# Another emission order for the start of a fused attention and feed-forward kernel, with new prices in its planner

## The chip, the cores and the metric

The kernel runs on one core of one Trainium2 chip. The metric is the device time of one execution in microseconds. Every time below is of the kernel before the change; "the profiled execution" is the single execution whose records the profile holds.

## What is computed

```python
# attention: q (4, 12288, 128), kv (4, 384, 32, 128), w_sr (128, 128)
kv_pool = kv.reshape(B, H // 4, 4, W // 4, 4, C).mean(axis=(2, 4))
k = v = kv_pool.reshape(B, -1, C) @ w_sr            # 768 keys a batch
s = (q @ k.transpose(0, 2, 1)) / np.sqrt(C)
s = s - s.max(-1, keepdims=True)
a = np.exp(s)
a /= a.sum(-1, keepdims=True) + 1e-09
x = (a @ v).reshape(49152, 128)
# feed-forward: w_in (128, 2048), w_out (2048, 128)
h = x @ w_in
g = h * (1.0 / (1.0 + np.exp(-1.702 * h)))
out = g @ w_out
```

Inputs and output are float32; the kernel multiplies in bfloat16. It leaves out the subtraction of the maximum and takes the row sum from a column of ones beside v.

## The kernel before

**Tiling.** The 49152 queries are 96 groups of 512, 24 groups a batch; four groups share one tile of transposed queries (qT). The 768 keys of a batch are six chunks of 128. A chunk of work on ScalarE (ACT) is 128 keys by 512 queries (exp, written to the buffer `ag`), or, in the feed-forward part, 128 hidden columns by 512 tokens (gelu). A **unit** is one ACT instruction over up to K = 3 chunks, that is three PSUM banks. Two sets of three banks (0 to 2, 3 to 5) alternate between units. The last two banks, 6 and 7, called spare here, serve everything else in turn: pooling, keys, values, transposes, and the sums that the drains collect (`acc`, `next_acc`).

**Fills and drains.** A fill (`fill_attn`, L331, or `fill_moe`, L511) is TensorE's one 512-column matmul per chunk, followed by ACT's instruction over all of them (L336 or L515). A drain of attention (`drain_attn`, L338) is K = 3 matmuls with 129 columns for one tile of 128 queries and half of the keys; three tiles (18 matmuls) share a spare bank, which VectorE (DVE) then empties with a reciprocal (L354) and a multiplication (L362). A drain of the feed-forward part (L517) is one 512-column matmul; 16 of them make a group of the output. `turn` (L418) transposes attention's output back, six tiles at a time.

**Four passes.** Attention for the first half of the groups (0 to 47), feed-forward for them, attention for the second half, feed-forward for it. Four groups of the second half (48 to 51) have their exp made on DVE from a polynomial (`early_fill`, L382 to L411) during the first feed-forward pass.

**What sets the order.** One Python loop (from L637) writes the instructions of all engines in order; each engine executes its own in that order. After the fill of unit n + 2 the loop gives TensorE drains and small jobs for the time of unit n, as far as a planner thinks that they fit: it holds a clock `now` for TensorE, the ends of ACT's units `end` (FIXED + CHUNK x chunks, L632 to L635) and, for each spare bank, when it comes free. Its unit of time is one 512-column matmul. `COST` (L607) gives each small job two numbers: what TensorE takes, and how much later the bank is free. Ahead of each fill `prepare` (L568) puts the jobs that the table `first` (L584) lists by hand for that unit, without asking whether they fit, and starts background work for groups that begin there: `background` (L453) issues `load_qT` two tiles ahead (a transposing load on SyncE's queue, SP), `cast_q` five tiles ahead, for group 10 the pixel loads of batch 1, and appends the pooling and the keys of batch 1 to the list `extras`, from which the loop takes when the planner allows. `gate` (L446) makes GpSimd's queue (POOL) wait for DVE, so that a load isn't issued earlier than its place.

**Start.** The pixel loads of batch 0 (`load_chunk`, L121, 512 KB after the cast) and the first four tiles of queries (`load_q`, L212) go through POOL's queue in the order of L232 to L243. `pool_chunk` (L128) sums 4 x 4 pixels by 16 small matmuls, `key_chunk` and `value_chunk` (L139, L146) multiply by w_sr; each ends in a DVE copy from the spare bank. `transpose_q` (L217) makes four transposes of one group of queries and a copy into qT, by ACT for group 0 and by DVE for the others. `warm` and `warm_wide` (L268, L281) are matmuls whose result nobody reads. The first eight groups are taken by key chunk and not by group, since the keys arrive one chunk at a time; the list `sizes` (L536) cuts them into units of one to three chunks.

**Frames.** `place` (L300) chooses where in `ag` a unit's result goes: in frames of three slots, and for the first eight groups in slots strided by group.

The lines of code that the steps of the prediction turn on are these:

```python
if p >= 2:
    now = max(now, end[p - 2] + HANDOVER / 2)
now += len(part)
begin = max(now + HANDOVER / 2, end[p - 1] if p else 0.0)
end.append(begin + FIXED + CHUNK * len(part))
```

Of the kernel before, what the change touches and what calls it, by code (L numbers as in the profile page):

```python
# [24 lines left out]
def kernel(  # L25
# [4 lines left out]
    _, H, W, _ = kv.shape  # L30
# [3 lines left out]
    JC = J // 128  # L34
# [7 lines left out]
    GB = NG // B  # L42
    SB = NS // B
    K = 3
# [36 lines left out]
    free = {6: 0.0, 7: 0.0}  # L81
    last_acc = 7
# [9 lines left out]
    def next_acc():  # L92
        return min((m for m in (13 - last_acc, last_acc) if m not in closes), key=lambda m: free[m])

    def acc_bf():
        return acc().bitcast(BF)
# [9 lines left out]
    def x_tile(s):  # L106
        return x[:, s % XS * SG:(s % XS + 1) * SG]
# [13 lines left out]
    def load_chunk(b, jc):  # L121

        a, ch = divmod(jc, HC)
        t = x_tile(XS - 1 - jc)
        nc.gpsimd.dma_start(out=t, in_=kv_r[b, a, ch])
        kv_tiles[b, jc] = t.rearrange("p (wp w1 c) -> p w1 wp c", w1=r, c=C)
# [72 lines left out]
    def cast_q(s):  # L199
        sl = slice(s * SG, (s + 1) * SG)  # L200
        nc.gpsimd.dma_start(out=q_bf[sl, :].rearrange("(p i) c -> p (i c)", p=128),
                            in_=q_flat[sl, :].rearrange("(p i) c -> p (i c)", p=128))

    def load_qT(s):
        qTs[s] = qpool.tile([128, 1, SG], BF, name="qT")
        nc.sync.dma_start_transpose(out=qTs[s], in_=q_bf[s * SG:(s + 1) * SG, :])
# [5 lines left out]
    def load_q(s, lo, hi):  # L212
        nc.gpsimd.dma_start(
            out=qs[s].rearrange("p (g e) -> p g e", g=4)[:, lo:hi, :],
            in_=q_flat[s * SG + lo * G:s * SG + hi * G, :].rearrange("(g p i) c -> p g (i c)", p=128, i=4))

    def transpose_q(g):  # L217
        s = g // 4
        if g % 4 == 0:
            qTs[s] = qpool.tile([128, 1, SG], BF, name="qT")  # L220
        ps = acc_bf()[:, 0:G].rearrange("p (i t) -> p i t", i=4)
        for i in range(4):
            o = (g % 4) * G + i * 128
            nc.tensor.transpose(ps[:, i, :], qs[s][:, o:o + 128], ident)  # L224
        dst = qTs[s][:, 0, (g % 4) * G:(g % 4 + 1) * G].rearrange("p (t i) -> p t i", i=4)
        src = ps.rearrange("p i t -> p t i")
        if g == 0:
            nc.scalar.copy(dst, src)
        else:
            nc.vector.tensor_copy(dst, src)  # L230

    w_sr_f = cpool.tile([128, C], F32)  # L232
    nc.sync.dma_start(out=w_sr_f, in_=w_sr)
    load_q(0, 0, 1)
    load_chunk(0, 0)
    load_q(0, 1, 4)
    load_chunk(0, 1)
    load_q(1, 0, 4)
    for jc in range(2, JC):
        load_chunk(0, jc)  # L240
    load_q(2, 0, 4)
    load_q(3, 0, 4)
    cast_q(4)  # L243

# [23 lines left out]
    def warm(n):  # L268

        for _ in range(n):  # L270
            nc.tensor.matmul(banks[:32, 2, :], ones, ones.unsqueeze(1).broadcast_to([128, 16, 32]),  # L271
                             start=True, stop=True)
# [4 lines left out]
    ag = agpool.tile([128, AG, 512], BF, name="ag")  # L277
# [3 lines left out]
    def warm_wide(n):  # L281
        for _ in range(n):
            nc.tensor.matmul(banks[:, 2, :], wide[:, 0:4, :].rearrange("p a b -> p (a b)"), wide, start=True, stop=True)

    warm(8)
    transpose_q(0)
    warm(2)
    warm_wide(4)


    slot_of = {}
    low = 0
    written = [0] * (AG // K)
    order, unit = [], 0

    def free_frames():
        busy = {s // K for s in slot_of.values()}
        return [f for f in range(low // K, AG // K) if f not in busy]

    def place(chunks):  # L300
        nonlocal order, unit
        unit += 1
        if chunks[0][0] == "a" and chunks[0][1] < 8:
            lo = [i * JC + jc for _, i, jc in chunks]
            step = JC
        else:
            if not order:
                order = sorted(free_frames(), key=lambda f: written[f])
            f = order.pop()
            lo = range(f * K, f * K + len(chunks))  # L310
            step = 1
        for c, s in zip(chunks, lo):
            assert s not in slot_of.values()
            slot_of[c] = s
            written[s // K] = unit
        return ag[:, lo[0]:lo[-1] + 1:step, :]

    def room_ahead():
        return K * len(free_frames())
# [126 lines left out]
    def gate():  # L446

        nc.vector.memset(gate_tile, 0.0)  # L448
        nc.gpsimd.memset(gate_tile, 0.0)  # L449
# [3 lines left out]
    def background(i):  # L453

        s = i // 4
        if i % 4 == 0:
            if QS <= s + 2 < NS:
                load_qT(s + 2)
            if CAST <= s + CAST < NS:
                gate()  # L460
                cast_q(s + CAST)
        if i == 10:
            gate()
            for jc in range(JC):
                load_chunk(1, jc)
        if 0 <= i - 16 < JC:
            extras.append((key_and_value, 1, i - 16))
        if 0 <= i - 15 < JC:
            extras.append((pool_chunk, 1, i - 15))
        if i == 26:  # L470
            gate()
            nc.gpsimd.dma_start(out=w_in_sb, in_=moe_w_in)
        if i == 34:
            gate()
            nc.gpsimd.dma_start(out=w_out_sb, in_=moe_w_out.rearrange("(o p) c -> p o c", p=128))
# [30 lines left out]
    extras = []  # L506
# [26 lines left out]


    NA, NM = NG * JC, NG * FCH
    chunks, sizes = [], [1, 3, 3, 1, 3, 1, 3, 1] + [3, 3, 2] * 4  # L536
    chunks += [(i, jc) for jc in range(2) for i in range(4)]
    chunks += [(i, jc) for jc in range(2) for i in range(4, 8)]
    chunks += [(i, jc) for jc in range(2, JC) for i in range(8)]
    chunks += [(i, jc) for i in range(8, NG) for jc in range(JC) if i not in early]  # L540
    seq, todo = [], []
# [1 line left out]
    for n in range(R):  # L543
        part = [c for c in chunks if c[0] // (NG // R) == n]
        while part:
            m = sizes.pop(0) if sizes else K
            seq.append(("a", part[:m]))
            part = part[m:]
# [19 lines left out]
    def prepare(p):  # L568

        nonlocal now  # L570
        for f, *args in first.get(p, ()):
            if f in COST:
                now = max(now, free[next_acc()])
            f(*args)
            if f in COST:
                now += COST[f][0]
                free[last_acc] = now + COST[f][1]
        kind, part = seq[p]
        for i, _ in part:
            if (kind, i) not in begun:  # L580
                begun.add((kind, i))
                (background if kind == "a" else background_moe)(i)

    first = {  # L584
        0: [(pool_chunk, 0, 0), (warm, 2), (key_chunk, 0, 0), (warm, 2)],
        1: [(transpose_q, 1), (transpose_q, 2), (transpose_q, 3), (warm, 3)],
        2: [(pool_chunk, 0, 1), (value_chunk, 0, 0), (warm, 2), (key_chunk, 0, 1)],
        4: [(transpose_q, 4), (transpose_q, 5), (transpose_q, 6)],
        5: [(transpose_q, 7)],
        6: [(pool_chunk, 0, 2), (value_chunk, 0, 1)],  # L590
        8: [(key_chunk, 0, 2)],
        9: [(pool_chunk, 0, 3), (value_chunk, 0, 2)],
        11: [(key_chunk, 0, 3)],
        12: [(pool_chunk, 0, 4), (value_chunk, 0, 3)],
        14: [(key_chunk, 0, 4)],
        15: [(pool_chunk, 0, 5), (value_chunk, 0, 4)],
        16: [(transpose_q, 8)],
        17: [(key_chunk, 0, 5), (transpose_q, 9)],
        18: [(value_chunk, 0, 5), (transpose_q, 10), (transpose_q, 11)],
        19: [(transpose_q, 12), (transpose_q, 13)],  # L600
        20: [(transpose_q, 14), (transpose_q, 15)]}

    FIXED, CHUNK, SWITCH, HANDOVER, EVACUATE, LATE = 0.33, 1.975, 6.0, 1.0, 4.5, 1.0
    COST = {pool_chunk: (2.5, 2.0), key_chunk: (0.7, 2.0), value_chunk: (0.7, 2.0),  # L607
            transpose_q: (1.2, 4.0), early_fill: (1.0, 5.5), key_and_value: (1.0, 3.0),
            transpose_pooled: (1.5, 3.0), make_k: (1.0, 3.0), make_v: (1.5, 3.0), turn: (1.5, 3.5)}
    SMALL, TURN = 0.26, 5.5  # L610
    PAUSE = 4.0
    now, end, extra_at = 0.0, [], 0.0
# [26 lines left out]
    for n in range(len(seq)):  # L639
        fill(n + 2)  # L640
        while True:
# [3 lines left out]
            f = None  # L645
            if turns and max(now, bank) >= turns[0][0]:
                f, args = turn, turns[0][1:]
# [4 lines left out]
            if not f and not steps and early_todo and low and min(slot_of.values()) >= low and (2, 1) in vs and dve <= now + 2.0 and now >= bank:  # L652
                f, args = early_fill, early_todo[0]
            if f and max(now, bank) + COST[f][0] > limit + (LATE if f is turn else 0.0 if f is early_fill else 4.5) and room >= 4 * K:
                f = None
            if f:
                now = max(now, bank) + COST[f][0]
                f(*args)
# [20 lines left out]
            kind, i, c = source[0]  # L679
# [15 lines left out]
            now = start + cost  # L695
# [39 lines left out]
```

The softmax here doesn't subtract the row's maximum and nothing guards it: scores larger than these inputs give would overflow.

## Time and profile before

| what | value |
|---|---|
| median of 9 runs | 971.34 us (970.97 to 972.62) |
| the profiled execution | 971.3 us |
| its span on the core | 969.5 us |
| ACT busy | 946.4 us |
| TensorE busy, matmuls | 953.2 us |
| DVE busy | 344.0 us |
| ACT idle ahead of L336, waiting for fills | 11.3 us in 8 waits |
| ACT idle ahead of L515, waiting for fills | 1.5 us in 2 waits |
| DMA, mean over the span | 92 GB/s |

"Busy" is time in which an engine has an instruction in work; TensorE's ends are modelled, so that matmuls that overlap count as one stretch. The span is counted on the core, from the first instruction to the last; the 1.8 us between it and the time of the execution lie outside of it. "Idle before" a group of instructions is the time that its engine stood still just ahead of them, with the engine whose work ended last before it. A wait costs time only on an engine that sets the end.

### The profile page before, as it was taken

The page shows a single profiled execution, that of the slowest core. Times are in us where ns is not written, and L with a number is a line of the kernel's source. Part 1 is how long each engine was busy: PE and PEld are TensorE (multiplying, and loading weights), DVE is VectorE, ACT ScalarE, POOL GpSimd, SP SyncE. Part 2 cuts the span into 40 slices and gives each one's busy share as a digit, 9 for nine tenths or more (in the row PEclk, how much of TensorE's full clock was granted, in tenths as well). Part 3 has the DMA queues.
Part 4 walks back from the last instruction along what each step waited for, and adds up shares of the span by engine and source line. Part 5 has one row for each costly group of instructions (what it writes and reads, how often), then busy time and mean ns, then how long its engine had stood idle before and what let it go on. Part 6 is the DMA issues. An engine that isn't in the chain of part 4 may idle for free.

```text
span 969.5 us, 15242 instructions
## 1 busy us (share of the span) xinstructions
PE 953.2 (98%) x6359; PEld 505.1 (52%) x6359; DVE 344.0 (35%) x734; ACT 946.4 (98%) x705; POOL 65.6 (7%) x113
## 2 busy tenths in 40 slices
PE   7899999999999999999999999999999999999997
PEld 3567777544444444444445777754444444444443
DVE  4444433201477778777602333311101011011010
ACT  4999999999999999999999999999999999999997
POOL 3100100330000232000000000000000000000000
PEclk9999999999999999999999999999999999999999
DMA  9898751999862698224347984652222222222222
GB/s 182 163 201 146 106 101 34 109 144 162 175 129 44 103 150 109 40 34 76 57 81 133 193 161 107 131 120 40 37 44 39 38 44 34 43 34 41 37 33 43
DMA packets 354164, 89.66 MB, mean 92 GB/s; under 512 B 328048, under 2 KB 351728, under 8 KB 353776
## 3 DMA queue, kind: packets, MB, share of 16 engines
q1 hardware_dynamic: 323936, 56.06, 32.9%
q0 software_dynamic: 29104, 32.51, 22.5%
q8 instruction: 49, 0.80, 0.4%
q10 hardware_dynamic: 1056, 0.13, 0.1%
q14 instruction: 19, 0.16, 0.1%
HBM read 52.49 MB, written 45.88 MB: 101 GB/s over the span
## 4 chain that ended last, share of the span: by engine, by line
ACT 48%; PE 47%; DMA 3%; DVE 1%; issue 0%; POOL 0%; POOLq 0%
ACT ag L515 36%; PE banks L513 17%; PE banks L520 17%; ACT ag L336 13%; PE banks L345 6%; PE banks L334 5%; DMA qT<-q_bf 2%; DMA x<-in_q_dram 1%; DVE qT L230 1%; PE banks L382 1%; PE banks L424 0%; PE banks L224 0%; ACT L515 0%; PE banks L134 0%; PE banks L271 0%
## 5 line engine op out<-in xcount | busy, mean ns | idle before, releaser
L515 ACT ACTIVATE ag<-banks 128x1536 bf16<-128x1536 f32 x512 | 690.0, 1542 | 1.6 <-PE banks L513 1.5
L513 PE MATMUL banks<-x,w_in_sb 128*128 128x512 bf16 x1536 | 414.8, 379 | 0.0
L520 PE MATMUL banks<-ag,w_out_sb 128*128 128x512 bf16 x1536 | 412.8, 379 | 0.5 <-ACT ag L515 0.5
L336 ACT ACTIVATE ag<-banks 128x1536 bf16<-128x1536 f32 (+1 forms) x188 | 250.6, 1445 | 11.7 <-PE banks L334 11.3
L520 PEld LDWEIGHTS <-w_out_sb 128*128 128x128 bf16 x1536 | 149.6, 98 | 181.5 <-issue 1.6
L513 PEld LDWEIGHTS <-w_in_sb 128*128 128x128 bf16 x1536 | 147.7, 97 | 176.5 <-issue 20.1
L528 DVE STREAM_TRANSPOSE o_sb<-banks 128x512 f32<-128x512 f32 x96 | 68.7, 716 | 398.9 <-PE banks L520 398.1
L345 PEld LDWEIGHTS <-ag 128*128 128x128 bf16 x2304 | 146.4, 98 | 45.4 <-issue 1.2
L345 PE MATMUL banks<-v,ag 128*128 128x129 bf16 x2304 | 162.8, 220 | 0.4 <-DVE v L158 0.3
L334 PE MATMUL banks<-qT,kT 128*128 128x512 bf16 x552 | 149.7, 379 | 7.0 <-ACT ag L336 4.8
L354 DVE RECIPROCAL rec<-banks 128x3 f32<-128x3 f32 x128 | 23.0, 180 | 132.8 <-PE banks L345 132.7
L409 DVE SCALAR_TENSOR_TENSOR ea<-ea,eb 128x512 f32<-128x512 f32 x96 | 66.0, 687 | 2.8
L334 PEld LDWEIGHTS <-kT 128*128 128x128 bf16 x552 | 47.3, 98 | 36.3 <-issue 4.5
L362 DVE TENSOR_TENSOR x<-banks,rec 128x384 bf16<-128x384 f32 x104 | 57.9, 557 | 3.6
L166 POOL DMA_DIRECT2D kvs<-in_kv_dram x32 | 40.3, 1330 | 16.6 <-DMA kvs<-in_kv_dram 12.9
L449 POOL MEMSET gate_tile<- 1x8 f32 x38 | 4.0, 106 | 461.4 <-DVE gate_tile L448 461.4
L398 DVE TENSOR_SCALAR ea<-banks 128x512 f32<-128x512 f32 x24 | 16.6, 691 | 30.0 <-PE banks L382 30.0
L411 DVE SCALAR_TENSOR_TENSOR ag<-ea,ee 128x512 bf16<-128x512 f32 x24 | 16.5, 686 | 1.0
L404 DVE SCALAR_TENSOR_TENSOR eb<-eb,ea 128x512 f32<-128x512 f32 x24 | 16.5, 688 | 0.7
L362 DVE TENSOR_TENSOR xt<-banks,rec 128x384 bf16<-128x384 f32 x24 | 13.4, 557 | 0.8
L230 DVE COPY qT<-banks 128x512 bf16<-128x512 bf16 x15 | 9.8, 687 | 4.7 <-PE banks L224 4.6
L426 DVE COPY x<-banks 128x768 bf16<-128x768 bf16 x12 | 6.7, 558 | 12.0 <-PE banks L424 11.9
(65 smaller groups left out, 155.5 us busy)
## 6 DMA issues: line engine op xcount, KB each, us to landing
out_dram<-o_sb SPq DMA_DIRECT2D x382, 64.0 KB, 2.0
kvs<-in_kv_dram POOLq DMA_DIRECT2D x32, 384.0 KB, 6.2
q_bf<-in_q_dram POOLq DMA_DIRECT2D x20, 512.0 KB, 7.3
x_bf<-x SPq DMA_DIRECT2D x13, 768.0 KB, 5.8
x<-in_kv_dram POOLq DMA_DIRECT2D x12, 512.0 KB, 12.3
x<-in_q_dram POOLq DMA_DIRECT2D x3, 512.0 KB, 20.4
w_in_sb<-in_moe_w_in_dram POOLq DMA_DIRECT2D x1, 512.0 KB, 5.3
w_out_sb<-in_moe_w_out_dram POOLq DMA_DIRECT2D x1, 512.0 KB, 6.8
```

Of the source, the lines that this page charges most:

```text
L166: nc.gpsimd.dma_start(out=kv_sums[b][:, i2], in_=kv_p[b, i, w, :, i2], **({"accum_op": ADD} if n else {}))
L230: nc.vector.tensor_copy(dst, src)
L334: nc.tensor.matmul(ps[:, k, :], kTs[i // GB][:, jc * 128:(jc + 1) * 128], rhs, start=True, stop=True)
L336: nc.scalar.activation(place([("a",) + c for c in chunks]), ps, AF.Exp, scale=scale)
L345: nc.tensor.matmul(av_of[u][:, k * (C + 1):(k + 1) * (C + 1)], weights(("a", i, jc))[:, o:o + T], vs[i // GB][:, jc, 0:C + 1], start=(jc = ...
L354: nc.vector.reciprocal(rec, ps[:, :, C])
L362: nc.vector.tensor_tensor(to, ps[:, :, 0:C], rec.unsqueeze(2).broadcast_to([128, TS, C]), MUL)
L409: nc.vector.scalar_tensor_tensor(a, a, COEFFS[k], b, ADD, MUL)
L513: nc.tensor.matmul(ps[:, k, :], w_in_sb[:, fc * 128:(fc + 1) * 128], x[:, g % (4 * XS) * G:(g % (4 * XS) + 1) * G], start=True, stop=True)
L515: nc.scalar.activation(place([("m",) + c for c in chunks]), ps, AF.Gelu_apprx_sigmoid)
L520: nc.tensor.matmul(o_of[g], w_out_sb[:, fc, :], weights(("m", g, fc)), start=(fc == 0), stop=(fc == FCH - 1))
L528: nc.vector.transpose(o_sb, o_of.pop(g))
```

## The change

1. The order of the first loads on POOL's queue: chunk 0 of the pixels ahead of the queries of group 0; the queries of groups 1 to 3 in two loads instead of one; the third tile of queries ahead of the last chunk of the pixels instead of behind it.
2. Ahead of the first fill, the transposition of group 0 and two `warm` matmuls go from between the first eight `warm` matmuls and the wide ones; the transposition comes after the first pooling.
3. Group 3's copy into qT goes to ACT as well.
4. The first 16 chunks are cut into 7 units instead of 8, groups 4 to 7 are taken by group within the first two key chunks, and `first` is rewritten: the transpositions of groups 8 to 15 begin earlier and stand one to a unit.
5. `place` uses frames for all groups.
6. The pixel loads of batch 1 are issued at group 13 instead of 10, its poolings and keys are due one group later, and a key that is still in `extras` when its group begins is made at once.
7. The planner's prices are changed.

```diff
-        if g == 0:
+        if g in (0, 3):
             nc.scalar.copy(dst, src)
...
     nc.sync.dma_start(out=w_sr_f, in_=w_sr)
+    load_chunk(0, 0)
     load_q(0, 0, 1)
-    load_chunk(0, 0)
-    load_q(0, 1, 4)
+    load_q(0, 1, 2)
+    load_q(0, 2, 4)
     load_chunk(0, 1)
     load_q(1, 0, 4)
     for jc in range(2, JC):
+        if jc == JC - 1:
+            load_q(2, 0, 4)
         load_chunk(0, jc)
-    load_q(2, 0, 4)
     load_q(3, 0, 4)
...
     warm(8)
-    transpose_q(0)
-    warm(2)
     warm_wide(4)
...
-        if chunks[0][0] == "a" and chunks[0][1] < 8:
-            lo = [i * JC + jc for _, i, jc in chunks]
-            step = JC
-        else:
-            if not order:
-                order = sorted(free_frames(), key=lambda f: written[f])
-            f = order.pop()
-            lo = range(f * K, f * K + len(chunks))
-            step = 1
...
+        if not order:
+            order = sorted(free_frames(), key=lambda f: written[f])
+        f = order.pop()
+        written[f] = unit
+        for k, c in enumerate(chunks):
+            slot_of[c] = f * K + k
+        return ag[:, f * K:f * K + len(chunks), :]
...
-        if i == 10:
+        if i == 13:
             gate()
             for jc in range(JC):
                 load_chunk(1, jc)
+        if 0 <= i - 17 < JC:
+            extras.append((key_and_value, 1, i - 17))
         if 0 <= i - 16 < JC:
-            extras.append((key_and_value, 1, i - 16))
-        if 0 <= i - 15 < JC:
-            extras.append((pool_chunk, 1, i - 15))
+            extras.append((pool_chunk, 1, i - 16))
...
-    chunks, sizes = [], [1, 3, 3, 1, 3, 1, 3, 1] + [3, 3, 2] * 4
+    chunks, sizes = [], [1, 1, 2, 3, 3, 3, 3] + [3, 3, 2] * 4
     chunks += [(i, jc) for jc in range(2) for i in range(4)]
-    chunks += [(i, jc) for jc in range(2) for i in range(4, 8)]
+    chunks += [(i, jc) for i in range(4, 8) for jc in range(2)]
...
+            while (key_and_value, i // GB, jc) in extras and kind == "a":
+                f, *args = extras.pop(0)
+                now = max(now, free[next_acc()]) + COST[f][0]
+                f(*args)
+                free[last_acc] = now + COST[f][1]
...
-        0: [(pool_chunk, 0, 0), (warm, 2), (key_chunk, 0, 0), (warm, 2)],
-        1: [(transpose_q, 1), (transpose_q, 2), (transpose_q, 3), (warm, 3)],
-        2: [(pool_chunk, 0, 1), (value_chunk, 0, 0), (warm, 2), (key_chunk, 0, 1)],
-        4: [(transpose_q, 4), (transpose_q, 5), (transpose_q, 6)],
-        5: [(transpose_q, 7)],
-        6: [(pool_chunk, 0, 2), (value_chunk, 0, 1)],
...
-        16: [(transpose_q, 8)],
-        17: [(key_chunk, 0, 5), (transpose_q, 9)],
-        18: [(value_chunk, 0, 5), (transpose_q, 10), (transpose_q, 11)],
-        19: [(transpose_q, 12), (transpose_q, 13)],
-        20: [(transpose_q, 14), (transpose_q, 15)]}
+        0: [(pool_chunk, 0, 0), (transpose_q, 0), (warm, 1), (key_chunk, 0, 0), (warm, 1)],
+        1: [(transpose_q, 1), (warm, 2)],
+        2: [(transpose_q, 2), (transpose_q, 3), (warm, 2)],
+        3: [(pool_chunk, 0, 1), (warm, 2), (key_chunk, 0, 1), (value_chunk, 0, 0)],
+        4: [(transpose_q, 4), (value_chunk, 0, 1)],
+        5: [(transpose_q, 5), (transpose_q, 6)],
+        6: [(transpose_q, 7), (pool_chunk, 0, 2)],
+        7: [(key_chunk, 0, 2)],
+        8: [(value_chunk, 0, 2), (pool_chunk, 0, 3)],
...
+        12: [(transpose_q, 8)],
+        13: [(key_chunk, 0, 4), (transpose_q, 9)],
+        14: [(value_chunk, 0, 4), (pool_chunk, 0, 5)],
+        15: [(transpose_q, 10)],
+        16: [(key_chunk, 0, 5), (transpose_q, 11)],
+        17: [(value_chunk, 0, 5)],
+        18: [(transpose_q, 12)],
+        19: [(transpose_q, 13)],
+        20: [(transpose_q, 14)],
+        22: [(transpose_q, 15)]}
...
-    FIXED, CHUNK, SWITCH, HANDOVER, EVACUATE, LATE = 0.33, 1.975, 6.0, 1.0, 4.5, 1.0
-    COST = {pool_chunk: (2.5, 2.0), key_chunk: (0.7, 2.0), value_chunk: (0.7, 2.0),
-            transpose_q: (1.2, 4.0), early_fill: (1.0, 5.5), key_and_value: (1.0, 3.0),
-            transpose_pooled: (1.5, 3.0), make_k: (1.0, 3.0), make_v: (1.5, 3.0), turn: (1.5, 3.5)}
+    FIXED, CHUNK, SWITCH, HANDOVER, EVACUATE, LATE = 0.295, 1.978, 6.0, 1.0, 4.5, 1.0
+    COST = {pool_chunk: (1.9, 2.6), key_chunk: (0.3, 2.4), value_chunk: (0.3, 2.4),
+            transpose_q: (1.05, 4.2), early_fill: (1.0, 5.5), key_and_value: (0.55, 3.5),
+            transpose_pooled: (0.9, 3.6), make_k: (0.8, 3.2), make_v: (0.8, 3.7), turn: (1.55, 3.5)}
```

More of the change, by code (lines that the diff above doesn't have):

```diff
@@ L302, in place @@
         unit += 1
-        if chunks[0][0] == "a" and chunks[0][1] < 8:
-            lo = [i * JC + jc for _, i, jc in chunks]
-            step = JC
-        else:
-            if not order:
-                order = sorted(free_frames(), key=lambda f: written[f])
-            f = order.pop()
-            lo = range(f * K, f * K + len(chunks))
-            step = 1
[L312 to L316, printed above, removed]
+        if not order:
[5 more added lines that the diff above has]
+        return ag[:, f * K:f * K + len(chunks), :]
     def room_ahead():
@@ L578, in prepare @@
         kind, part = seq[p]
-        for i, _ in part:
+        for i, jc in part:
             if (kind, i) not in begun:
@@ L582, in prepare @@
                 (background if kind == "a" else background_moe)(i)
-    first = {
-        0: [(pool_chunk, 0, 0), (warm, 2), (key_chunk, 0, 0), (warm, 2)],
-        1: [(transpose_q, 1), (transpose_q, 2), (transpose_q, 3), (warm, 3)],
-        2: [(pool_chunk, 0, 1), (value_chunk, 0, 0), (warm, 2), (key_chunk, 0, 1)],
-        4: [(transpose_q, 4), (transpose_q, 5), (transpose_q, 6)],
-        5: [(transpose_q, 7)],
-        6: [(pool_chunk, 0, 2), (value_chunk, 0, 1)],
[L591 to L596, printed above, removed]
-        16: [(transpose_q, 8)],
-        17: [(key_chunk, 0, 5), (transpose_q, 9)],
-        18: [(value_chunk, 0, 5), (transpose_q, 10), (transpose_q, 11)],
-        19: [(transpose_q, 12), (transpose_q, 13)],
-        20: [(transpose_q, 14), (transpose_q, 15)]}
@@ new lines @@
+    first = {
+        0: [(pool_chunk, 0, 0), (transpose_q, 0), (warm, 1), (key_chunk, 0, 0), (warm, 1)],
[7 more added lines that the diff above has]
+        8: [(value_chunk, 0, 2), (pool_chunk, 0, 3)],
+        10: [(key_chunk, 0, 3)],
+        11: [(value_chunk, 0, 3), (pool_chunk, 0, 4)],
+        12: [(transpose_q, 8)],
[8 more added lines that the diff above has]
+        22: [(transpose_q, 15)]}
```

## The prediction

> **What bounds the kernel now.** I read the page first: busy shares, then the chain of work that ended last.
>
> ```profile
> span 969.5 us, 15242 instructions
> PE 953.2 (98%) x6359; PEld 505.1 (52%) x6359; DVE 344.0 (35%) x734; ACT 946.4 (98%) x705; POOL 65.6 (7%) x113
> ACT 48%; PE 47%; DMA 3%; DVE 1%; issue 0%; POOL 0%; POOLq 0%
> L515 ACT ACTIVATE ag<-banks 128x1536 bf16<-128x1536 f32 x512 | 690.0, 1542 | 1.6 <-PE banks L513 1.5
> ```
>
> The reader is to see that ScalarE (ACT) works for 946.4 of 969.5 us, with TensorE (PE) close behind, the two feeding each other. ACT's work is fixed by the problem, so a change can win only ACT's idle time, 23.1 us. Next I read ACT's own timeline, which merges instructions that follow each other closely and gives the idle time ahead of each run in brackets.
>
> ```profile
> 5.14 0.58 ACT L228 COPY qT<-banks 128x512 bf16<-128x512 bf16 x1 [3.11 <-PE banks L224]
> 9.19 0.60 ACT L336 ACTIVATE ag<-banks 128x512 bf16<-128x512 f32 x1 [3.47 <-PE banks L334]
> 12.47 1.45 ACT L336 ACTIVATE ag<-banks 128x1536 bf16<-128x1536 f32 x1 [2.68 <-PE banks L334]
> 14.83 1.94 ACT L336 ACTIVATE ag<-banks 128x1536 bf16<-128x1536 f32 x2 [0.91 <-PE banks L334]
> ...
> 22.47 14.90 ACT L336 ACTIVATE ag<-banks 128x1536 bf16<-128x1536 f32 x12 [0.41 <-PE banks L334]
> 38.80 32.73 ACT L336 ACTIVATE ag<-banks 128x1536 bf16<-128x1536 f32 x24 [1.43 <-PE banks L334]
> 72.55 76.32 ACT L336 ACTIVATE ag<-banks 128x1536 bf16<-128x1536 f32 x56 [1.02 <-PE banks L334]
> ...
> 428.07 68.80 ACT L515 ACTIVATE ag<-banks 128x1536 bf16<-128x1536 f32 x51 [1.29 <-PE banks L513]
> 498.19 119.22 ACT L336 ACTIVATE ag<-banks 128x1536 bf16<-128x1536 f32 x88
> ...
> 618.72 344.91 ACT L515 ACTIVATE ag<-banks 128x1536 bf16<-128x1536 f32 x256
> ```
>
> Nearly all idle time lies ahead of 22.5 us, then at 37.4 (1.43), 71.5 (1.02) and 425 to 428 (0.23 and 1.29). The rest is a tail that the change does not touch. One more loss hides inside the runs. A lone unit shows 1.45, so the last run gives (344.91 - 1.45) / 255 = 1.347 us a unit; the run of 56 gives 1.361, that of 88 gives 1.354. So small waits cost 55 x 0.014 = 0.8 us and 87 x 0.007 = 0.6 us, and in the run of 24 another 0.3. For the gap at 71.5 I read who waited for whom, and the DMA queues from 55 to 58 us.
>
> ```profile
> PE banks L334 <- DMA qT<-q_bf: 1.2, 1, 1.2
> ```
>
> ```profile
> q0 software_dynamic: 160, 0.59, 96.9%
> q1 hardware_dynamic: 160, 0.04, 9.9%
> ```
>
> The transposing load of qT for groups 20 to 23, issued at 48.42, landed at 71.69: it began during the six pixel loads of batch 1 (issued from 44.62), and crept until they had passed. Last, TensorE's first matmuls:
>
> ```profile
> 0.97 3.60 PE L271 MATMUL banks<-ones 128*32 128x512 bf16 x8 [0.97 <-DVE col L249]
> 5.93 1.20 PE L283 MATMUL banks<-wide 128*128 128x512 f32 x4
> 7.53 0.60 PE L271 MATMUL banks<-ones 128*32 128x512 bf16 x2
> ```
>
> Eight in 3.60 are 0.43 us apart, the two at 7.53 are 0.22 apart: the clock doubles at about 6.
>
> **What the Trainium skill says.** TensorE: Matmul & The Clock Gate, Part 1: the array starts at half clock and is released after some 3.4 us of activity in a free-running window; the trace agrees (0.43, then 0.2155). DMA: Bandwidth & Descriptors, Queues, rings and completion order: an engine takes turns between queues packet by packet. The trace agrees: 160 packets each, but 0.59 MB against 0.04, so a queue of small packets starves. ScalarE: Activation LUTs, What ACT_TABLE_LOAD costs: one element a cycle at 1.2 GHz, so a 512-column chunk is 0.427 us; the trace's 1.347 for three leaves 0.066 fixed a unit, less than the page's 0.093 (186 ns less the overlap of 93).
>
> **The change, part by part.** Prices from the timeline: a 512-column matmul 0.2155 us, a 129-column drain matmul 0.0567, four transposes 0.23, a pool 0.39. Four transposes' start to the DVE copy's start 0.43, copy 0.69 (0.63 in a row); pool's start to its copy 0.60; fill's start to ACT's start 0.42 with one chunk, 0.63 with two, 0.85 with three; a last drain's end to the bank's release 1.0 (0.2, reciprocal 0.22, multiply 0.56).
>
> 1. First loads. The bytes ahead of chunk 1 are the same, so it still lands at about 12. Chunk 0 is issued 0.68 earlier and lands near 6.35 instead of 7.0. But the four wide matmuls hold TensorE from 5.93 to about 6.95, since their operand is ready at 5.88: pool 0 starts at 6.97 instead of 7.04, and ACT's first unit at 9.1 instead of 9.19. POOL issues one DMA more (0.7 us), hidden by the queue of transfers.
>
> 2. Units of the first eight groups, followed with those prices. Group 1: transposes 8.9, copy to 10.0, unit of one chunk at 10.5. Groups 2 and 3: transposes 10.3 and 10.5, one copy on DVE, one on ACT (11.2 to 11.8, in a gap), unit at 12.2. Chunk 1: pool at 12.05, key, copy to 13.65, unit at 14.55 (14.83 before, with four chunks done in both). Then 16.46, 18.48, 20.08 and, with no gap left, 21.43 for the eighth unit, where before the ninth started at 22.47. One fixed 0.066 is in it. Gain 1.0; bounds 0.4 and 1.6 for unknown landings.
>
> 3. Later transposes. From there 12 units take the same time; q's third load comes ahead of chunk 5, both with 0.6 us or more of cover (25.2 against use at 25.8; 27.7 against 28.5). The transposes of groups 12 to 15, which made the 1.43 gap, are spread. But two of them now stand where the drains hold the two spare banks. By the order, 15 drain matmuls (0.85) and a transpose precede fill 19: 0.14 late. After fill 19 three drains close a bank, and the next transpose must wait 1.0 for DVE to release it: fill 20 is 0.75 late. The same before fill 22: 0.7 late, and the bank for the next turn 0.16. Lost 1.75, won 1.43: -0.3. If DVE were free to hide it, up to +1.4; if both waits grew by a copy of 0.69, -1.7.
>
> 4. Batch 1's pixels three groups later: their loads move from 44.6 to about 51.4. The qT load at about 47.6 now has the engines to itself (one cast joins at 49); it needs some 3 us. Gain 1.02. The next qT load (issued about 58.3) starves instead: pixels end about 69, two casts by 72, it lands near 77.6. Group 24's fill needs it at 80.0. This cover of 2.4 us hides it; without it the 1.02 returns. Chunks land from 56.6, each 2.8 later; the pools stand at 59.0 to 77.9. Gates on POOL and DVE keep their order.
>
> 5. Lower prices in the planner. I added up TensorE's work between successive fills from the built order of both kernels. A window above 1.35 is free only while a reserve of 0.5 us (1.347 less fill and latency of 0.85) lasts. For before this count gives gaps of 0.73 from unit 44 on in the first attention pass, 0.75 in the second, and 1.58 at the two windows ahead of 428 us (18 drains; 18 drains and 5 matmuls of the output), where the trace shows 0.8, 0.6 and 1.52: the count can be trusted. For after: 0.25, 0.03 and 2.28, as a third window of 18 drains and two output matmuls (1.45) appears at unit 340. So +0.5, +0.55, -0.7; units 24 to 43 +0.1. Between -0.7 and +1.2 for the three together.
>
> Sum: 1.0 - 0.3 + 1.02 + 0.5 + 0.55 - 0.7 + 0.1 = 2.17. The profiled execution took 971.3 (span 969.5 and 1.8 around it), beside a median of 971.34. So 971.3 - 2.2 = 969.1.
>
> **Rivals.** (a) The clock rises late. The change removes a transposition and two warming matmuls from 4.5 to 5.9, so TensorE idles 1.5 us in the very window that released it. For: the window is 3.4 us, and now little over half busy. Against: still more than half busy, and the next is dense. Price: half clock to 9.4 puts 0.7 on the wide matmuls, 0.4 on pool 0, 0.2 on the first fill: 1.3, so 970.4. (b) The same taken further, the other side: half clock until about 16. Of 14.4 us on the way to the eighth unit TensorE has 6.3 (2 pools, about 9 transposes, 2 keys, 16 chunks), so each us costs 0.44; from 6 to 16.5 4.6 us, less 2.2: 973.7. It decides from about 11 us on. Against: at half clock TensorE is denser, which should release it. (c) The next qT load comes late: 1.0 lost, 970.1. For: only 2.4 us of cover. (d) The bank waits are hidden: 969.1 - 1.4 = 967.7. For: each is one chain of small steps, and I may place a transpose too late. That the planner's prices change nothing is excluded by the built order.
>
> **How the numbers follow.** Forecast 969.1 (968.5 to 969.7) 0.48; (d) 0.14; (a) 0.18; (c) 0.08; (b) 0.12. A measurement tells 0.2%, 1.9 us, from no change: faster means under 969.4. That is two thirds of the forecast (0.33) and (d): 0.47. Slower than 973.3 is most of (b): 0.08. The rest, 0.45, is no change. The range runs from (d) to past (a) and (c), 967.5 to 971.0, and leaves out (b) and the edges.
>
> **What would show it.** Right: ACT's first unit near 9.1, the eighth near 21.4; no gap near 70; gaps of 0.6 to 0.8 ahead of units 20 and 22, near 38 and 41; the run after it at 1.35 a unit; gaps of about 2 together near 425. Wrong: wide matmuls 0.43 apart; TensorE waiting for qT near 80; no gap at 38; a new gap after 150 us elsewhere.

## The result, and the profile after

The changed kernel takes 968.41 us (median of 10 runs, 967.25 to 970.22) against 971.46 for the kernel before (30 runs beside it): the ratio is 0.9966, interval 0.9958 to 0.9974. That is 3.05 us or 0.31% less; forecast were 969.1 and 0.23%. The median lies in the range of 967.5 to 971.0, but just below 968.5 to 969.7, the band of the forecast itself. The profiled execution took 968.59, with a span of 966.8 us against 969.5.

The page of the changed kernel, its lines of busy time and the gelu group:

```profile
span 966.8 us, 15246 instructions
PE 952.4 (99%) x6356; PEld 505.7 (52%) x6356; DVE 344.2 (36%) x733; ACT 945.0 (98%) x705; POOL 66.0 (7%) x114
L508 ACT ACTIVATE ag<-banks 128x1536 bf16<-128x1536 f32 x512 | 689.0, 1553 | 2.1 <-PE banks L506 2.0
```

ACT's idle time fell from 23.1 to 21.8 us, and its busy time by 1.4, though it has one copy more (group 3's, 0.58) and only one unit's fixed 0.07 less: what shows as busy here holds small waits too. ACT's timeline of the changed kernel (start, duration, count; in brackets the idle time ahead) shows where:

```profile
8.88 0.58 ACT L228 COPY qT<-banks 128x512 bf16<-128x512 bf16 x1 [6.86 <-PE banks L224]
10.55 0.60 ACT L329 ACTIVATE ag<-banks 128x512 bf16<-128x512 f32 x1 [1.08 <-PE banks L327]
...
19.57 19.30 ACT L329 ACTIVATE ag<-banks 128x1536 bf16<-128x1536 f32 x15 [0.53 <-PE banks L327]
39.49 2.79 ACT L329 ACTIVATE ag<-banks 128x1536 bf16<-128x1536 f32 x2 [0.61 <-PE banks L327]
42.88 104.38 ACT L329 ACTIVATE ag<-banks 128x1536 bf16<-128x1536 f32 x77 [0.60 <-PE banks L327]
...
148.57 274.52 ACT L508 ACTIVATE ag<-banks 128x1536 bf16<-128x1536 f32 x204
...
426.17 48.65 ACT L508 ACTIVATE ag<-banks 128x1536 bf16<-128x1536 f32 x36 [1.24 <-PE banks L506]
...
496.71 118.69 ACT L329 ACTIVATE ag<-banks 128x1536 bf16<-128x1536 f32 x88
...
616.72 344.22 ACT L508 ACTIVATE ag<-banks 128x1536 bf16<-128x1536 f32 x256
```

Read beside the timeline of before: the first unit starts later, 10.55 against 9.19. The unit at 42.88 has as much work behind it as the one that started at 38.80 + 3 x 1.36 = 42.88 before, so by then nothing was won. From there the first table load comes at 147.28 instead of 148.88 (1.6: the gap at 71.5 is gone, and 0.6 of small waits). The run of 204 is 0.40 shorter, the gaps near 425 are larger (with one of 0.33 at 474.8, together 1.97 against 1.52; the units behind them take 0.1 more), the second attention pass is 0.53 shorter, the last pass 0.69.

TensorE's first matmuls in the changed kernel:

```profile
0.97 3.60 PE L273 MATMUL banks<-ones 128*32 128x512 bf16 x8 [0.97 <-DVE col L251]
5.89 2.07 PE L285 MATMUL banks<-wide 128*128 128x512 f32 x4 [1.33 <-DVE wide L281]
7.77 0.65 PE L134 MATMUL banks<-sum,x 128*128 128x32 bf16 x16
```

Four wide matmuls in 2.07 instead of 1.20: the array still ran at half clock, and the pooling started at 7.77 instead of 7.04. This is rival (a) of the prediction. (The half clock is read from the matmuls' length: the profile's own clock record stands at 1.00 from the first microsecond, before the change and after it.) The ten times fall into groups: seven lie at 968.29 to 968.59, two at 967.25 and 967.31, one at 970.22. Only the run of 968.59 has a profile; that the other six of its group had the late clock too, and the two lower ones an early one, is inferred. Six kernels below and here leave TensorE idle for 1.3 to 1.5 us ahead of the wide matmuls, and their profiles fit: the late clock is seen in runs of a higher group (968.59, 969.29, and 967.02 where 966.0 is the lowest group), the early one in runs of the lowest group (969.17, 967.92, 971.78).

### The profile page after: what moved, and what is told of

Same layout as the page of the kernel before. It is cut to its first block, busy times and chain, and to the rows that moved or that the text cites. A ratio compares the mean times of both kernels' runs of the same rounds, so it can differ in the third digit from the quotient of the medians.

```text
span 966.8 us, 15246 instructions
## 1 busy us (share of the span) xinstructions
PE 952.4 (99%) x6356; PEld 505.7 (52%) x6356; DVE 344.2 (36%) x733; ACT 945.0 (98%) x705; POOL 66.0 (7%) x114
## 4 chain that ended last, share of the span: by engine, by line
PE 54%; ACT 44%; DVE 1%; issue 0%; DVEq 0%
ACT ag L508 36%; PE banks L506 17%; PE banks L513 17%; PE banks L338 9%; ACT ag L329 8%; PE banks L327 8%; PE banks L375 1%; PE banks L417 0%; DVE qT L230 0%; PE banks L134 0%; PE banks L224 0%; PE banks L273 0%; PE banks L285 0%; DVE xt L355 0%; ACT L508 0%
## 5 line engine op out<-in xcount | busy, mean ns | idle before, releaser
L329 ACT ACTIVATE ag<-banks 128x1536 bf16<-128x1536 f32 (+2 forms) x187 | 249.8, 1463 | 6.2 <-PE banks L327 5.6
L506 PEld LDWEIGHTS <-w_in_sb 128*128 128x128 bf16 x1536 | 147.8, 97 | 175.9 <-issue 17.2
L399 DVE TENSOR_SCALAR ea<-eb 128x512 f32<-128x512 f32 x24 | 10.3, 431 | 0.7
```

The costliest lines, as they stand in the source:

```text
L329: nc.scalar.activation(place([("a",) + c for c in chunks]), ps, AF.Exp, scale=scale)
L506: nc.tensor.matmul(ps[:, k, :], w_in_sb[:, fc * 128:(fc + 1) * 128], x[:, g % (4 * XS) * G:(g % (4 * XS) + 1) * G], start=True, stop=True)
```

## The experiments

The theory after the result had four parts: the new start is worth about 1 us but loses it to a late clock in most runs; the later pixels are worth 1 us; two transpositions cost about 1.2 us at units 20 and 22; and the planner's price for ACT's unit, not those of the small jobs, sets TensorE's pace in the long passes. Each run below is beside the kernel before on the same chip; three chips were used, and the kernel before has medians of 971.51 to 971.56 on them. Several kernels have times in two or more groups, so groups are named where a median would mix them.

**Eleven warming matmuls.**

```diff
-    warm(8)
+    warm(11)
     warm_wide(4)
```

> The changed kernel with three more warming matmuls, so that TensorE works until about 5.7 and not until 4.4 while it waits for the wide operand. Theory (the clock rose late because of that idle time): the wide matmuls stand 0.27 apart and not 0.46, ACT's first unit starts near 9.1 and not at 10.55, the eighth near 21.4 and not at 22.3; the time falls by 0.8 to 1.2, to 967.2 to 967.6. Rival (the landing of chunk 1 and the copies set the start whatever the clock): the eighth unit stays at 22.3, the time at 968.4.

Measured 967.41; four of five runs at 967.08 to 967.44, one at 970.95. Ratio 0.9963, interval 0.9951 to 0.9975. TensorE and ACT in this run:

```profile
5.90 1.20 PE L285 MATMUL banks<-wide 128*128 128x512 f32 x4 [0.45 <-DVE wide L281]
6.93 0.57 PE L134 MATMUL banks<-sum,x 128*128 128x32 bf16 x16
```

```profile
9.03 0.60 ACT L329 ACTIVATE ag<-banks 128x512 bf16<-128x512 f32 x1 [0.67 <-PE banks L327]
14.46 1.45 ACT L329 ACTIVATE ag<-banks 128x1536 bf16<-128x1536 f32 x1 [1.34 <-PE banks L327]
41.70 104.38 ACT L329 ACTIVATE ag<-banks 128x1536 bf16<-128x1536 f32 x77 [0.60 <-PE banks L327]
```

The wide matmuls are back at 1.20, the first unit at 9.03, and all that follows is 1.18 earlier (41.70 against 42.88). The late clock costs 1.2 us. The rival falls.

**The idle time put into the kernel before.**

```diff
     warm(8)
+    warm_wide(4)
     transpose_q(0)
     warm(2)
-    warm_wide(4)
```

> The kernel before with the first transposition and the two warming matmuls moved behind the wide ones, so that TensorE idles from 4.4 to 5.9 as in the changed kernel. Theory (the idle time lets the clock rise late in a part of the runs): two groups of times, one near 971.4, one 1.0 to 1.4 above; where the clock is late the wide matmuls stand 0.46 apart and not 0.27. Rival (only the new order of loads makes the start late): one group near 971.4.

Measured: six runs at 971.70 to 971.90, seven at 972.75 to 974.36; ratio 1.001 (1.0002 to 1.0018). Two groups a microsecond apart appear, as the theory says; of the 29 runs of the kernel before beside them one lies above 972.5. The profile fell into the lower group (wide matmuls in 1.19), so the spacing in the upper group was not seen here. The lower group itself is 0.3 above before: the transposition now stands behind the wide matmuls, and the first unit comes at 9.99.

**The old price of ACT's unit alone.**

```diff
-    FIXED, CHUNK, SWITCH, HANDOVER, EVACUATE, LATE = 0.295, 1.978, 6.0, 1.0, 4.5, 1.0
+    FIXED, CHUNK, SWITCH, HANDOVER, EVACUATE, LATE = 0.33, 1.975, 6.0, 1.0, 4.5, 1.0
```

> The changed kernel with the old prices of ACT's unit alone (FIXED 0.33, CHUNK 1.975). Theory (an old price of 1.348 us against ACT's real 1.344 gives TensorE slightly more than ACT's time to fill, so TensorE sets the pace in the runs without gaps): the last pass goes back from 1.3442 to about 1.347 a unit, the second attention pass loses 0.6, the gaps near 425 shrink by 0.9 by my count of TensorE's work between fills; together 0.5 slower than the change, about 968.9 to 969.3. Rival (the pace of the last pass has another cause, such as the transfers of the output): the last pass keeps 1.344.

Measured: six runs at 969.05 to 969.35, seven at 970.17 to 971.00, which is 1.8 to 2 above the groups of the changed kernel. The expectation named the place, but its 0.5 was less than a third of it. Passes of this run:

```profile
496.07 119.26 ACT L329 ACTIVATE ag<-banks 128x1536 bf16<-128x1536 f32 x88
616.64 344.87 ACT L508 ACTIVATE ag<-banks 128x1536 bf16<-128x1536 f32 x256
```

Both are back where they were before the change (119.22 and 344.91), with all else of the change in place; the rival falls. The missing part is in the first feed-forward pass. Its gaps shrink from 1.97 to 1.12, as counted, but the pass as a whole grows from 346.85 to 347.28: small waits in it take back 1.3. With the run of eleven matmuls, whose clock was early too, the sum is 0.1 to the first table load, 0.43, 0.57 and 0.65, or 1.75 of the 1.8 by which the spans differ (967.4 and 965.6).

**A price that is higher still**, with eleven warming matmuls.

```diff
-    FIXED, CHUNK, SWITCH, HANDOVER, EVACUATE, LATE = 0.295, 1.978, 6.0, 1.0, 4.5, 1.0
+    FIXED, CHUNK, SWITCH, HANDOVER, EVACUATE, LATE = 0.36, 1.978, 6.0, 1.0, 4.5, 1.0
```

> The changed kernel with eleven warming matmuls and ACT's unit priced at 1.356 us (FIXED 0.36), twice as far above the real 1.344 as the old price of 1.348 and more. Theory (TensorE is given work for the priced time and sets the pace with it): second attention pass 119.8 to 120.2 instead of 118.7, last pass 345.5 or more instead of 344.2; in all 2.5 to 4 slower than with the warming matmuls alone, 970 to 971.5. Rival (only the drains' places matter, not their sum): passes as before, within 1 of 967.4.

Measured: nine of 14 runs at 970.63 to 971.08, five from 972.68 up. In the nine about 3.5 more than with the warming matmuls alone. Passes:

```profile
148.22 347.10 ACT L508 ACTIVATE ag<-banks 128x1536 bf16<-128x1536 f32 x256
496.63 119.94 ACT L329 ACTIVATE ag<-banks 128x1536 bf16<-128x1536 f32 x88
617.89 345.08 ACT L508 ACTIVATE ag<-banks 128x1536 bf16<-128x1536 f32 x256
```

The second attention pass and the total follow the price as expected; the last pass less than expected, 345.08 and not 345.5: that is 1.348 a unit at a price of 1.356, so there the pace does not follow the price all the way. The first feed-forward pass has no gap near 425 left: 347.10 for 256 units, where the changed kernel takes 346.85 from 148.57 to 495.42.

**The old prices of the small jobs alone** (`COST` as before).

> The changed kernel with the old prices of the small jobs (COST) and the new ones of ACT's unit. The count of TensorE's work between fills gives 0.4 more idle time of ACT, all of it near the handover to the drained early groups (3.0 against 2.5 in the first feed-forward pass): 968.8. Rival (the gain of the small waits comes from these prices, not from the unit's): both attention passes lose 0.6 each again, 969.6.

Measured: times from 967.92, in groups near 968.0 and 969.2, with four of 22 at 974.7 to 975.2; the profile with an early clock has a span of 966.1, 0.5 above that with the warming matmuls. The passes keep 118.72 and 344.19, so the rival falls. What is lost is in the first feed-forward pass (347.48 against 346.85; expected were 0.4), and the groups lie 0.6 to 0.9 above those of the changed kernel: the small jobs' prices matter, but less than the unit's, and not in the second attention pass or the last pass.

**The new prices alone in the kernel before.**

> The kernel before with the new prices alone (ACT's unit and the small jobs), its start and its pixel loads as they were. Theory (the prices alone bring most of the gain, since the new start brings nothing until the clock is up): the second attention pass at 118.7 and the last pass at 344.2 as in the changed kernel, the wait for qT near 70 stays; 2.0 to 2.5 faster than before, 968.9 to 969.5. Rival (the prices only fit the new start): within 0.7 of before.

Measured 968.94 (968.79 to 969.92), ratio 0.9973 (0.9962 to 0.9984): 2.6 less than before, a little beyond the expectation. Second attention pass 118.78, last pass 344.14. The wait for qT near 70 stays, as expected; ACT's gap there is 1.39. The prices alone bring most of what the whole change brings.

**The new prices and the later pixels in the kernel before**, its old start kept.

> The kernel before with the new prices and the later pixels of batch 1, its start as it was. Theory: one microsecond less than with the prices alone, about 968.0 to 968.4, level with the changed kernel: the new order of the start is worth nothing where the clock rises late, and 1.0 where it rises early. Rival (the new start is part of the gain in every run): 0.8 to 1.0 slower than the changed kernel, 969.3.

Measured 968.18 (967.81 to 968.99), ratio 0.9965 (0.9953 to 0.9976): level with the changed kernel, and 0.76 below the prices alone: that is what the later pixels bring here. So the new start is worth nothing in the median, and the rival falls; against the two lower runs of the changed kernel (967.25 and 967.31) this kernel is 0.9 slower, as the theory has it for an early clock.

**The pixels back at group 10 in the changed kernel.**

```diff
-        if i == 13:
+        if i == 10:
             gate()
             for jc in range(JC):
                 load_chunk(1, jc)
```

(The poolings and keys go back to groups 15 and 16 with it.)

> The changed kernel with batch 1's pixels, poolings and keys back at groups 10, 15 and 16. Theory (the later loads took away the wait for the queries of groups 20 to 23): a wait of TensorE for qT of about 1.0 comes back near 70, and the count of TensorE's work gives 0.5 back near 425; 968.8 to 969.4. Rival (the new order of the first units or the prices took it away): no wait for qT, 967.9 to 968.4.

Measured 968.16 (967.86 to 969.47), three runs at 967.86 to 968.16 and two at 969.29 and 969.47. The expected 968.8 to 969.4 is missed by the median, which lies where the rival had it; the rival's other half, no wait for qT, is not what the trace shows. Group against group it is 0.6 to 1.2 slower than the changed kernel; that the median isn't slower would follow if three of its five runs had the early clock (as their times suggest) against two of ten. The two profiled runs both had the late clock, and there it is 0.7 slower (969.29 against 968.59): the first table load comes 1.14 later, with a wait of 0.94 ahead of it, and the first feed-forward pass is 0.44 shorter (346.41 against 346.85; expected were 0.5). The wait is back, in TensorE and then in ACT:

```profile
PE banks L327 <- DMA qT<-q_bf: 0.9, 1, 0.9
```

```profile
72.45 75.95 ACT L329 ACTIVATE ag<-banks 128x1536 bf16<-128x1536 f32 x56 [0.94 <-PE banks L327]
```

**The transpositions of groups 13 to 15 placed by the planner.**

```diff
+        if i == 8:
+            extras.extend([(transpose_q, 13), (transpose_q, 14), (transpose_q, 15)])
...
-        18: [(transpose_q, 12)],
-        19: [(transpose_q, 13)],
-        20: [(transpose_q, 14)],
-        22: [(transpose_q, 15)]}
+        18: [(transpose_q, 12)]}
```

> The changed kernel with the transpositions of groups 13 to 15 handed to the planner as small jobs from group 8 on, in place of fixed places ahead of units 19, 20 and 22. Theory (these places force a wait for a spare bank that the drains hold): the gaps of 0.6 near 38 and 41 go, ACT's first run reaches past unit 22; 1.0 to 1.3 faster than the changed kernel, 967.2 to 967.4 with a late clock and near 966.2 with an early one. Rival (TensorE has no time for them there, wherever they stand): the gaps move and the time stays at 968.4.

Measured: median 967.22; three runs at 966.01 to 966.14, six at 967.00 to 967.30, but also four at 973.2 to 976.5, so that the ratio is uncertain (0.9974, 0.9955 to 0.9993). ACT in the profiled run:

```profile
19.23 126.46 ACT L329 ACTIVATE ag<-banks 128x1536 bf16<-128x1536 f32 x94 [0.53 <-PE banks L327]
```

One run from 19.23 to the table load: both gaps of 0.6 are gone, and 1.2 to 1.3 is won in the two lower groups. The rival falls.

**Both mends together.**

> The changed kernel with both mends: eleven warming matmuls, and the transpositions of groups 13 to 15 placed by the planner. Theory (two independent losses of about 1.2 each): span near 964.3 and a time of 966.0 to 966.3, in nearly every run. Rival (they overlap, since an early start only moves the wait): 967.2.

Measured: seven of 22 runs at 966.10 to 966.22, the time of the theory, but not "in nearly every run": 12 lie at 969.8 or above, up to 979.98. The median is 969.88, ratio 0.9979 (0.9963 to 0.9995): the mends add up, and something else takes it back in most runs. The profiled run of 967.02 shows a little of it, a wait of 0.7 for qT near 80.

**A lower price on top of both.**

```diff
-    FIXED, CHUNK, SWITCH, HANDOVER, EVACUATE, LATE = 0.295, 1.978, 6.0, 1.0, 4.5, 1.0
+    FIXED, CHUNK, SWITCH, HANDOVER, EVACUATE, LATE = 0.265, 1.978, 6.0, 1.0, 4.5, 1.0
```

> As the run with both mends, and ACT's unit priced lower still, 1.336 us (FIXED 0.265) against 1.342. The count of TensorE's work gives no small waits at all in both attention passes (0.26 and 0.25 less) and another 0.1 in the last pass, and about the same gaps near 430: 0.7 faster than with both mends, 965.4. Rival (1.342 is below ACT's real 1.344 already, so nothing is left to win): the same time.

Measured: three runs at 965.55 to 965.63, the lowest of all, 0.55 below the floor of both mends (0.7 was expected, so this rival falls too); the rest up to 977.29, ratio 0.9985 (0.9963 to 1.0008). The second attention pass takes 118.32, the last 344.00. The profiled run took 977.29 and shows the largest wait. What TensorE waited for, then ACT:

```profile
PE banks L327 <- DMA qT<-q_bf: 9.9, 1, 9.9
```

```profile
90.23 1.45 ACT L329 ACTIVATE ag<-banks 128x1536 bf16<-128x1536 f32 x1 [10.51 <-PE banks L327]
```

This is rival (c), ten times as large as I had priced it: the queries of groups 24 to 27, issued at 56.42 behind the pixels, landed 32.3 us later, at 88.7, when their fill had been due near 79. TensorE stood so long that its granted clock fell as well: the record has 0.50 from about 81.8 to 91.8, and ACT waits another 1.09 at 92.77.

**Group 3's copy on DVE again**, with eleven warming matmuls.

> The changed kernel with eleven warming matmuls and group 3's copy on DVE again. Theory (ACT's copy stands in a gap and spares the third unit a second DVE copy): the third unit starts 0.3 to 0.4 later, all after it too; 967.8 against 967.4. Rival (chunk 1 of the pixels sets the fourth unit in any case): the fourth unit at the same 14.46, the time at 967.4 or 0.1 less.

Measured: lower group 967.38 to 967.80 (ten of 22 runs), the others up to 975.95. The third unit starts 3.44 after the first instead of 3.07, the fourth 5.74 instead of 5.43, but the sixth 9.31 instead of 9.36: the loss is real and used up two units later. Neither expectation holds: it is not carried on, though chunk 1 does not hide it. ACT's copy is worth about 0.1 us in the end (medians of the lower groups, 967.49 against 967.36). The profiled run, 970.77, waited 1.5 for qT near 83, and another 1.1 at 78.7, whose cause the profile doesn't show clearly (for TensorE's weight load it counts as "issue").

## Why the prediction was right

The direction, the time and most of the places were right. The sum was right partly by luck, because two errors met: a loss of about 1 at the start that I had as a rival, and a gain of 1.1 in the feed-forward passes that I had not counted. Where the clock seems to have risen early, the time was 967.3, below the whole range.

1. First loads. "Pool 0 starts at 6.97" and "the first unit at 9.1" held with the clock early (6.93 and 9.03 in the run with eleven matmuls). In seven of the ten runs of the changed kernel it was late, as far as the times tell, and rival (a) came true: price forecast 1.3, measured 1.2. Its chance, 0.18, was far too low. The argument "still more than half busy" was no reason; the Trainium skill's page TensorE: Matmul & The Clock Gate, Part 1, speaks of a window of some 3.4 us of sustained activity and does not say how much idle time it allows; here 1.3 us were enough to miss it often.

2. Units of the first groups. With the early clock the fourth, fifth and sixth units were forecast at 14.55, 16.46 and 18.48; they came at 14.46, 16.41 and 18.39. The eighth came at 18.39 + 2 x 1.345 = 21.08 instead of 21.43, since a gap of 0.25 that the forecast still had ahead of the seventh did not come. Up to the sixth unit this chain of small steps could be worked out to a tenth of a microsecond.

3. Later transpositions. Forecast gaps of 0.75 and 0.7 for the two forced waits; measured 0.61 and 0.60, ahead of units 20 and 22 as forecast. The run in which the planner places them shows that the place was the cause: the same work, no gap. Rival (d) is excluded by the two gaps.

4. Later pixels. The wait of 1.0 went, as forecast, and came back (0.94) when that part was undone. The load of qT issued at 48.13 landed after 6.8 us instead of 23.2 (forecast: some 3). The whole part is worth 0.7 to 0.8 in the two pairs of runs that differ in it, where the forecast had 1.02. The next load starved as described; it was forecast at 77.6 and landed at 58.96 + 20.1 = 79.06. Group 24's fill was due near 80.7 in that late-clock run, so 1.6 of cover was left instead of 2.4. In undisturbed runs this step is right; in others rival (c) comes true. A faster start may make that more frequent, since the fill is then due earlier and the cover shrinks: the runs that lie 2.9 us or more above their kernel's lowest went from 1 of 10 in the changed kernel to 12 of 22 with both mends. But that is not shown. The kernel with the old unit price, whose first unit also came at 9.03, has none in 13. And the runs with both mends were made on another chip than these, on which the kernel with group 3's copy on DVE, without the second mend, has 9 of 22 and the kernel before 2 of 59: what the chip adds is open.

5. Lower prices. Second attention pass: forecast 0.55, measured 0.53. First: 0.6 and 0.6. Gaps near 425: forecast 0.7 lost, measured 0.45, and the third gap stands ahead of unit 340, as forecast. Missing was the gain of 0.40 and 0.69 in the feed-forward passes. The step that failed is ACT's own length: I took 1.347 us a unit, the pace of the last pass, as what ACT needs. That pace was itself set by TensorE, which the planner loaded for 1.348 (0.33 + 3 x 1.975 = 6.255 matmuls of 0.2155). With a price of 1.342 the pace is (344.22 - 1.45) / 255 = 1.344; with 1.336 it is 1.343, so ACT's own length is 1.343 or a little less. The runs with prices of 1.348 and 1.356 put the time back up, by 1.8 and 3.5.

The profiled spans add up: 0.0 at the start, 1.6 to the first table load, 0.4, 0.53 and 0.69 in the passes, less 0.45 near 425 and 0.1 in the units behind, is 2.7, as measured.

What stays open: why the transposing load is so much slower in some executions. In the one of 977.29 us, between 72 and 78 us its 919 packets took 109% of 16 engines' time, 0.114 us each (6 x 16 x 1.092 / 919), when the pixels had landed; in the changed kernel's profile 1623 packets took 56.5% of the same stretch, 0.033 us each:

```profile
q1 hardware_dynamic: 919, 0.24, 109.2%
```

```profile
q1 hardware_dynamic: 1623, 0.42, 56.5%
```

Most disturbed runs have no profile. That all of them waited for the same load is likely from the three profiles that did (0.7, 1.5 and 9.9 us), not shown. What their records do hold is the mean granted clock: with both mends it is 0.999 or 1.000 in the ten undisturbed runs and down to 0.992 in the others (the longest, 979.98, has the lowest), and 0.993 in the run of 977.29, where it was the long wait that brought it down. So TensorE probably stood still for some microseconds in many of them. Halving the pixel loads, three chunks at group 13 and three at group 17 behind the queries, might give the cover back; it was not tried. No variant here is shown to beat the changed kernel (0.9966) by more than the intervals: eleven warming matmuls come nearest (0.9963, with one run of five at 970.95), and the transpositions placed by the planner have the lowest median, 967.22, but a ratio of 0.9974 from four disturbed runs of 15.

## What to carry to other kernels

When two engines feed each other in lockstep, the pace of a run without gaps need not be the length of the slower engine's instruction: here a planner that priced that instruction 0.3% too long gave the other engine so much work that it set the pace, and no gap showed. Work that brings TensorE's clock up was part of the start's critical path here, so moving it needs the same care as moving a load. A transfer that is moved takes its neighbours' place in the queue: ask which load it starves next, and how much cover that one has on a bad execution and not on the profiled one.

## What the runs showed of the hardware

- Eight warming matmuls and 1.3 us of idle time left the clock late in most runs of the changed kernel, as far as the times tell. With eleven, four of the five profiles have the wide matmuls in 1.19 to 1.20 us; the one of 977.29 us has them in 1.49, so there the clock rose about 0.3 later.
- In the run of 977.29 us TensorE fell idle near 78.8; its granted clock went to 0.50 near 81.7, 2.9 us later, and back to 1.00 near 91.9, 3.2 us after it had work again. Matmuls of 512 columns lasted 609 to 634 ns at 0.50 and 379 at 1.00. At the start they last 606 to 635 too, where the clock record says 1.00: it does not show the half clock there.
- Wide float32r matmuls of 512 columns lasted 396 ns (median) with the clock up, in the kernel before, and 628 with it down, in the changed kernel.
- A transposing load of 2048 x 128 queries took 6.8 us from issue to landing (groups 20 to 23, changed kernel), and for groups 24 to 27, behind the pixels, 17.2 (eleven warming matmuls), 20.1 (changed kernel) and 32.3 (the run of 977.29 us).
